# Attention and mixture of experts on one core: weight sums moved ahead of the signs, and four adds of the last pair moved from GpSimd to VectorE

## The chip, the cores and the metric

One core of one Trainium2 chip runs the whole kernel in one launch. The metric is the device time of an execution in microseconds (us); less is better. TensorE is called PE in the profile (PEld is its weight load), VectorE DVE, ScalarE ACT, GpSimd POOL and SyncE, which issues most DMAs, SP.

## What is computed

The inputs are `q`, `k`, `v` of shape (4, 8, 768, 64): four batches, eight heads, 768 tokens, 64 features. Attention is restricted by a hash, and a layer of eight experts follows:

```
bits   = (q @ proj > 0), (k @ proj > 0)        # 6 signs per token
mask   = bucket(q bits) == bucket(k bits)
scores = where(mask, q @ k.T / 8, -1e9)
attn   = softmax(scores)                       # over the keys
x      = (attn @ v), heads side by side        # 3072 tokens x 512
e      = argmax(x @ w_gate + modality_bias)    # one of 8 experts per token
out    = gate_weight * (relu(x @ w1[e]) @ w2[e])
```

## The kernel before, in words

**Attention.** The 32 heads are taken in 16 pairs, numbered 0 to 15; the variable `i` is the pair, `NPR` is 16 and `NT` is 6, the number of tiles of 128 tokens. The loop over pairs at the end of `attention` is software-pipelined. While pair `i` is scored and weighed, pair `i + 1` has its row maxima taken and pair `i + 2` is transposed and gets its hash signs. The order of TensorE's work inside a pair is written out by hand as six strings, one per key tile (`PLAN`; `PLAN0` for pair 0 and `LAST` for pair 15), and each letter is one step:

- S: a step of `score` (L410, L411): matmuls of one head's scores, 512 or 2 x 256 columns, into a PSUM bank; ScalarE takes the exponential into `pb` (L430, L444). From the second key tile on, the weights `pb` of each head are added up over the key tiles in `sp` (L447). There are ten such adds per pair, two for each of the key tiles 1 to 5. GpSimd does them; in pair 15 head 0 is on GpSimd and head 1 on VectorE (`spd=(15,)`).
- M: a step of `maxp` (L344, L350): matmuls whose row maxima VectorE takes (L346, L352). Two PSUM buffers.
- T: `turn`, three steps of transposes (L303), and as the fourth step `signs`: sixteen matmul instructions on tiles of 64 rows x 32 columns (L220) that write the two banks `psu`, and two VectorE comparisons that read these banks (L231).
- A: a third of `weigh`: two key tiles of weighted sums of `v` (L463), on tiles of 128 rows x 64 columns, into the same two banks `psu`. The first of a pair's three steps opens the banks with L457, which so has to wait for the comparisons of L231.
- Q: `sums(i - 1)`: four matmuls (eight instructions) on tiles of 128 rows x 32 columns (L486) that fold `sp` of the pair before into denominators, and one VectorE add into `gs` (L491). They read the result of the last adds of L447.
- V, v: sums of `v`. F, f, E, e, x, y: steps of `finish` and `finish_x`, which close a batch every four pairs, route its tokens and write rows of a table with indirect DMAs of GpSimd (L784). R: residues (L311, L312). B: the broadcast of maxima (L374 to L378). L, l: loads.

The order on TensorE in attention is fixed by these strings. On VectorE, ScalarE, GpSimd and SP a scheduler puts the instructions in order, by the order of emission and what each waits for; some are tied with `behind` or `after`, which order two instructions without a semaphore. `marks` holds the instructions that later code ties to.

**The seam.** `body` then starts the experts. The first slot `("e", 0)` (496 tokens of one expert, all from the first three batches) is prepared while pair 15 still runs: SP loads its rows of the table, GpSimd issues four gathers (L949), and `xprep` transposes the gathered rows in four chunks `c` of 128 features (L967), rounds them on ScalarE (L970) and takes the residue on VectorE (L974). The transposes of chunks 0 and 1 are tied behind the weighing of key tile 3, those of chunks 2 and 3 behind that of key tile 5, and the last third of the weighing behind the transposes of chunk 1. The experts' weights come as `raw`, are rounded by ScalarE (L929), and their residue is taken by VectorE or, for every second one of the first eight, by GpSimd (L933). The first matrix product is L985 to L987, the second L1026 to L1028. `finish(B - 1)`, which begins with `sums(NPR - 1)`, runs interleaved with this slot. Here the order on TensorE too is the scheduler's.

The lines that the change touches are the two plans, L447 in `score`, the letter Q in the loop of `attention` (L643), and the residue in `xprep` (L974).

Of the kernel before, what the change touches and what calls it, by code (L numbers as in the profile page):

```python
# [10 lines left out]
F32 = mybir.dt.float32  # L11
# [4 lines left out]
ALU = mybir.AluOpType  # L16
# [4 lines left out]
NT = S // 128  # L21
# [8 lines left out]
CFG = dict(spd=(15,), fxs=3, wy=(0.3, 0.71), hpf=0, he=0, hn=0, hm=0, avp=(1, 2, 3, 4, 5, 6), avs=(2,), early=2, w3=(0, 0.9), x3=(0, 1), nmd=1, man=(), man0=2, hpo=0, hpe=0, p0=(0, 1), p1=(0, 0.25), p2=(0, 0.4), p3=(0.4, 0.9), s0=4, rc='DDDD', rq=(1, 2), tq=(3, 3, 1, 1, 0, 0), wh=(0.5, 0.78), ws=(0.78, 1.05), n2=2, psx=2, psm=2, pss=2, npb=6, ut=8, qk=4, v=2, wm=(0, 0.9), wf=(0.04, 1.02), wx=(0.3, 0.71), sub="DPPD", fx='D', fx3='R', raw=4, wp=7, LS=4, LL=7, pn=8, rv=(0,), rs='DDPP', r1=(0, 0.5), r2=(0, 1), avg=1, fub=2, fd=2, pm=(), fj=0, fxe=1.0)  # L30
# [2 lines left out]
GROUP = 2  # L33
PLAN = (
    "yMSTSTMSM",
    "STEeLfvxMAVSSMMTxfe",
    "eySMSMlARRQfMSFMyF",
    "SRMSeMSMx",
    "SFfEMSfMRSMF",
    "fSMRSMMEBABSe",  # L40
# [9 lines left out]
LAST = (  # L50
    "SySS",
    "SevAVSSe",
    "eySSAQSy",
    "SSeS",
    "SSS",
    "SSASe",
# [32 lines left out]
def chain(*gens):  # L89
    for g in gens:  # L90
        yield from g


def attention(ctx, actx, tc, a, x_d, l_d, route=None, setup=None, before_last=None):
    nc = tc.nc
    q, k, v, proj = a["q"], a["k"], a["v"], a["proj"]
    NPR = a.get("npair", NP)
# [308 lines left out]
    marks = {}  # L406
# [6 lines left out]
    def score(i):  # L413

        t = st[i]
        t["sp"] = spool.tile([P, 2, S], F32, name="sp")
        t["pb"] = [pbuf[(NT * i + kt) % NPB] for kt in range(NT)]

        banks = [0]

        def bank(shape):
            banks[0] += 1
            if i == NPR - 1 and banks[0] % 2:
                return ps_m.tile(shape, F32, name="psm")
            return ps_s.tile(shape, F32, name="pss")

        def main(kt, h):
            sp = bank([P, MAIN])
            scores(t, sp, h, kt, COLS[0])
            marks["p"] = nc.scalar.activation(t["pb"][kt][:, h, 0:MAIN], sp, AF.Exp, scale=0.125).ins  # L430

        if i == 0:
            for kt in range(NT):
                main(kt, 0)
                yield
        for kt in range(NT):
            pb = t["pb"][kt]
            for h in range(int(i == 0), 2):
                main(kt, h)
                yield  # L440
            sp = bank([P, 2, REST])
            for h in range(2):
                scores(t, sp[:, h], h, kt, COLS[1])
            nc.scalar.activation(pb[:, :, MAIN:S], sp, AF.Exp, scale=0.125)  # L444
            if kt > 0:
                for h in range(2):
                    marks["add"] = (nc.vector if h and i in CFG["spd"] else nc.gpsimd).tensor_tensor(out=t["sp"][:, h], in0=(t["pb"][0] if kt == 1 else t["sp"])[:, h], in1=pb[:, h], op=ALU.add).ins  # L447
            yield

    def weigh():  # L450
# [135 lines left out]
    with tc.manual_schedule(engines={mybir.EngineType.PE}):  # L586
        load(1)
        load_v(0)
        load(2)
        constants()  # L590
        with tc.manual_schedule(engines={mybir.EngineType.DVE, mybir.EngineType.Activation, mybir.EngineType.Pool}):
            opening = first()
        wg = sm.tile([P, 4, 8], F32, name="wg", bufs=1)
        nc.sync.dma_start(out=wg, in_=a["moe_w_gate"].rearrange("(c p) e -> p c e", p=P))
        gst = fconst.tile([P, 4, 32], F32, name="gst")
        nc.gpsimd.memset(gst, 0.0)
        nc.gpsimd.tensor_copy(out=gst[0:64, :, 0:8], in_=wg[0:64])
        nc.gpsimd.tensor_copy(out=gst[64:128, :, 16:24], in_=wg[64:128])
        ones = fconst.tile([P, 4, 32], F32, name="ones")
        nc.gpsimd.memset(ones, 0.0)  # L600
        for c in range(4):
            nc.gpsimd.memset(ones[:, c, c:c + 1], 1.0)
        if setup is not None:
            setup()
        for nm in spread_to.values():
            nc.gpsimd.memset(nm.bitcast(F32), 0.0)
        avs = weigh()
        fins = xs = iter(())
        late = []
        for i in range(NPR):  # L610
            ss = score(i) if i else opening
            ms = maxp(i + 1, late) if i + 1 < NPR else iter(())
            ts = chain(turn(i + 2), signs(i + 2)) if i + 2 < NPR else iter(())
            rs = residues(i + 2) if i + 2 < NPR else iter(())
            if i % 4 == 0 and i > 0:
                fins = finish(i // 4 - 1)
            if i % 4 == 2 and i > 4:
                xs = finish_x(i // 4 - 1, 0, NT)
            for kt in range(NT):
                if i == NPR - 1 and kt == 1:  # L620
                    before_last(ps_x.tile([P, MAIN], F32, name="psx"))
                if i == NPR - 1 and kt < 3:
                    next(xs, None)
                    next(xs, None)
                for c in (PLAN0 if i == 0 else LAST if i == NPR - 1 else PLAN)[kt]:
                    if c == "S":
                        next(ss)
                    elif c == "M":
                        next(ms, None)
                    elif c == "T":  # L630
                        next(ts, None)
                    elif c == "R":
                        next(rs, None)
                    elif c == "A":
                        next(avs)
                    elif c == "B":
                        if late:
                            late.pop(0)()
                    elif c == "v":
                        vadds(i)  # L640
                    elif c == "V":
                        vsums(i)
                    elif c == "Q":  # L643
                        if i > 0:
                            sums(i - 1)
                    elif c == "L":
                        if i + 3 < NPR:
                            load(i + 3)
                    elif c == "l":
                        if i + 1 < NPR:  # L650
                            load_v(i + 1)
                    elif c == "F" and i % 4 == 0 or c == "f" and i % 4 == 1:
                        next(fins, None)
                    elif c == "e" and i % 4 >= 2 or c == "E" and i == NPR - 2:
                        next(fins, None)
                    elif c == "x" and i % 4 == 2 or c == "y" and i % 4 == 3:
                        next(xs, None)
                        next(xs, None)
        for _ in avs:
            pass  # L660
# [9 lines left out]
SL = sum(GW)  # L670
# [214 lines left out]
def experts(ctx, tc, a, x_d, tab, out, ps_x, idents, fold, marks):  # L885
    nc = tc.nc
# [16 lines left out]
    def after(ins, other):  # L903
        tc.add_manual_dep(ins, other.name, mybir.DependencyInfo(mybir.DependencyClass.NoSync, mybir.DependencyReason.DATA), reason="the first slot follows the last pair's steps")

    def nt(s):
        return 1 if s[0] == "s" else TS // P
# [44 lines left out]
    def xprep(s, xg, dst):  # L952

        xh = xp.tile([P, 4, TS], F32R, name="xh")
        xl = xp.tile([P, 4, TS], F32R, name="xl")
        dst += [xh, xl]
        if nt(s) == 1:
            tp = ps_x.tile([P, 4, P], F32, name="psx")
            for c in range(4):
                nc.tensor.transpose(tp.bitcast(F32R)[:, c], xg[:, 0, c * P:(c + 1) * P], identr)  # L960
            nc.scalar.copy(out=xh[:, :, 0:P], in_=tp)
            nc.vector.tensor_tensor(out=xl[:, :, 0:P], in0=tp, in1=xh[:, :, 0:P].bitcast(F32), op=ALU.subtract)
            return
        for c in range(4):
            tp = ps_x.tile([P, TS], F32, name="psx")
            for g in range(nt(s)):
                tr = nc.tensor.transpose(tp.bitcast(F32R)[:, g * P:g * P + GW[g]], xg[0:GW[g], g, c * P:(c + 1) * P], identr[0:GW[g], 0:GW[g]])  # L967
                if s == ("e", 0):
                    after(tr.ins, marks["u", 3 if c < 2 else 5])
            cp = nc.scalar.copy(out=xh[:, c, 0:SL], in_=tp[:, 0:SL])  # L970
            if s == ("e", 0) and c == 1:
                after(marks["U", 4], tr.ins)
                after(marks["ut"], cp.ins)
            nc.vector.tensor_tensor(out=xl[:, c, 0:SL], in0=tp[:, 0:SL], in1=xh[:, c, 0:SL].bitcast(F32), op=ALU.subtract)  # L974
            if c % 2:
                yield

# [268 lines left out]
```

## Time and profile before

| | us |
|---|---|
| median of 3 runs | 759.83 (759.24 to 761.26) |
| the profiled execution's own time | 760.22 |
| its span, first to last instruction | 758.1 |
| PE busy | 738.9 |
| DVE busy | 499.9 |
| POOL busy | 440.9 |
| ACT busy | 363.8 |

Times in the profile are counted from the start of the span. Pairs take some 26 to 29 us each; pair 15 ends at about 457 us, and the experts fill the rest. Matmuls are pipelined and their ends are modelled, so the distance from the start of one to the start of the next tells more than their durations. A row that stands for several instructions (x8) gives the time from the first one's start to the last one's end.

### The profile page before, as it was taken

Reading aid. Unit: us, or ns where it says so; the run is one execution under the profiler, and the core shown is the slowest. Engines: PE = TensorE matmul, PEld = TensorE weight load, DVE = VectorE, ACT = ScalarE, POOL = GpSimd, SP = SyncE. Lnnn points to the kernel's source line nnn. Section 1 sums busy time; section 2 is a strip of 40 time slices with the busy share of each in tenths; the row PEclk is TensorE's granted clock in tenths of the full one; section 3 lists DMA queues with packets and bytes.
Section 4 is the critical chain, followed back from the end, with each engine's and each line's share of the span. In section 5 each row is a group of like instructions: output and inputs, shape, how many; then the busy total and the mean of one; then the engine's idle time right before and its main releaser. Section 6 shows DMA issues by size and latency. Waiting matters only on the chain.

```text
span 758.1 us, 12219 instructions
## 1 busy us (share of the span) xinstructions
PE 738.9 (97%) x4308; PEld 523.4 (69%) x4308; DVE 499.9 (66%) x878; ACT 363.8 (48%) x649; POOL 440.9 (58%) x339
## 2 busy tenths in 40 slices
PE   6899999999999999999999999999999999999995
PEld 3556576566666657666666656888888877788884
DVE  6997779789877887977987877654343442334423
ACT  5446565555555555556465454343343432424333
POOL 8598779769888769887869984712222202202011
PEclk9999999999999999999999999999999999999998
DMA  9464455345676435664324163556544764434332
GB/s 187 116 142 109 113 122 140 83 106 116 111 131 162 105 91 133 121 157 124 92 69 85 61 199 112 115 207 185 159 137 139 250 214 147 141 123 139 96 113 82
DMA packets 105832, 99.26 MB, mean 131 GB/s; under 512 B 62594, under 2 KB 82978, under 8 KB 105760
## 3 DMA queue, kind: packets, MB, share of 16 engines
q1 hardware_dynamic: 99616, 83.79, 43.6%
q0 software_dynamic: 4832, 12.94, 4.9%
q10 hardware_dynamic: 1312, 1.65, 0.9%
q8 instruction: 36, 0.59, 0.4%
q14 instruction: 36, 0.29, 0.2%
HBM read 59.33 MB, written 12.94 MB: 95 GB/s over the span
## 4 chain that ended last, share of the span: by engine, by line
PE 81%; issue 9%; DMA 3%; POOL 2%; SPq 1%; DVE 1%; ACT 1%; POOLq 0%; ACTq 0%
PE psu L463 17%; PE pss L410 9%; PE pss L411 8%; PE psm L344 5%; PE hps L985 5%; PE hps L986 5%; PE hps L987 5%; PE yps L1026 4%; PE yps L1027 4%; PE yps L1028 4%; PE psm L350 3%; PE psx L303 2%; PE psx L486 2%; PE psx L548 2%; PE psu L220 1%
## 5 line engine op out<-in xcount | busy, mean ns | idle before, releaser
L447 POOL TENSOR_TENSOR sp<-sp,pb 128x768 f32<-128x768 f32 x124 | 225.3, 1851 | 14.1 <-ACT pb L444 13.4
L346 DVE TENSOR_REDUCE mx<-psm 128x1 f32<-128x512 f32 x192 | 130.0, 687 | 22.2 <-PE psm L344 19.1
L430 ACT ACTIVATE pb<-pss 128x512 f32<-128x512 f32 x186 | 111.5, 600 | 58.7 <-PE pss L411 50.2
L463 PE MATMUL psu<-pb,vt 128*64 128x512 f32 (+1 forms) x768 | 136.1, 497 | 0.0
L933 DVE TENSOR_TENSOR w<-raw,w 128x1024 fp32r<-128x1024 f32 x52 | 66.9, 1287 | 97.9 <-ACT w L929 97.3
L463 PEld LDWEIGHTS psu<-pb,vt 128*64 128x64 f32 x768 | 51.3, 137 | 70.6 <-issue 60.9
L929 ACT CAST w<-raw 128x1024 fp32r<-128x1024 f32 x56 | 58.5, 1047 | 81.4 <-PE yps L1028 76.7
L444 ACT ACTIVATE pb<-pss 128x512 f32<-128x512 f32 x93 | 55.6, 598 | 82.3 <-PE pss L411 80.0
L1096 POOL DMA_INDIRECT out<-y,tb x25 | 24.6, 984 | 104.1 <-ACT y L1095 100.4
L447 POOL TENSOR_TENSOR sp<-pb,pb 128x768 f32<-128x768 f32 x31 | 56.2, 1835 | 45.2 <-ACT pb L444 45.2
L1026 PE MATMUL yps<-w,hl 128*128 128x512 f32 x200 | 79.5, 397 | 0.0
L1027 PE MATMUL yps<-w,hh 128*128 128x512 f32 x200 | 78.1, 391 | 0.0
L1028 PE MATMUL yps<-w,hh 128*128 128x512 f32 x200 | 78.0, 390 | 0.0
L949 POOL DMA_INDIRECT xg<-x_d,tb x17 | 18.4, 1084 | 98.1 <-DMA tb<-tab 94.4
L985 PE MATMUL hps<-xh,w 128*128 128x496 f32 x192 | 74.4, 388 | 0.0
L986 PE MATMUL hps<-xl,w 128*128 128x496 f32 x192 | 73.8, 384 | 0.0
L987 PE MATMUL hps<-xh,w 128*128 128x496 f32 x192 | 73.8, 384 | 0.0
L410 PE MATMUL pss<-m_0g,s_0g 128*128 128x512 f32 (+1 forms) x186 | 69.2, 372 | 0.0
L991 DVE SCALAR_TENSOR_TENSOR hl<-hps,hh 128x496 fp32r<-128x496 f32 x48 | 32.4, 674 | 53.0 <-ACT hh L990 52.9
L352 DVE TENSOR_REDUCE mx<-psm 128x2 f32<-128x512 f32 x96 | 66.1, 688 | 1.0
L410 PE MATMUL pss<-m_1g,s_1g 128*128 128x512 f32 (+1 forms) x186 | 65.7, 353 | 0.2 <-ACT pb L430 0.2
L990 ACT ACTIVATE hh<-hps 128x496 fp32r<-128x496 f32 x48 | 28.1, 585 | 78.5 <-PE hps L987 76.1
(267 smaller groups left out, 1419.7 us busy)
## 6 DMA issues: line engine op xcount, KB each, us to landing
raw<-moe_w SPq DMA_DIRECT2D x56, 512.0 KB
vt<-v SPq DMA_DIRECT2D x16, 384.0 KB
qk<-q SPq DMA_DIRECT2D x31, 192.0 KB
qk<-k SPq DMA_DIRECT2D x31, 192.0 KB
x_d<-xs SPq DMA_DIRECT2D x18, 256.0 KB
tw<-moe_w SPq DMA_DIRECT2D x2, 2048.0 KB
m_0g<-m_0g SPq DMA_DIRECT2D x16, 192.0 KB
s_0g<-s_0g SPq DMA_DIRECT2D x16, 192.0 KB
```

What stands on the lines that cost most here:

```text
L346: marks["m"] = nc.vector.tensor_reduce(out=mx[:, qt + j, hi, 0:1], in_=mp, axis=AX.X, op=ALU.max).ins
L410: nc.tensor.matmul(out, t["s1"][h][:, ks], t["m1"][h][:, cs], start=True, stop=False)
L430: marks["p"] = nc.scalar.activation(t["pb"][kt][:, h, 0:MAIN], sp, AF.Exp, scale=0.125).ins
L447: marks["add"] = (nc.vector if h and i in CFG["spd"] else nc.gpsimd).tensor_tensor(out=t["sp"][:, h], in0=(t["pb"][0] if kt == 1 else t["s ...
L463: marks["u", kt] = nc.tensor.matmul(t["u"][part][64 * h:64 * h + 64, 0:w], t["v"][:, h, kt], t["pb"][kt][:, h, COLS[part]], start=False, s ...
L933: (nc.gpsimd if n < 8 and n % 2 else nc.vector).tensor_tensor(out=lo, in0=r, in1=hi.bitcast(F32), op=ALU.subtract)
L985: nc.tensor.matmul(hps, lo[:, c, fs], xh[:, c, 0:SL], start=(c == 0), stop=False)
L986: nc.tensor.matmul(hps, hi[:, c, fs], xl[:, c, 0:SL], start=False, stop=False)
L987: nc.tensor.matmul(hps, hi[:, c, fs], xh[:, c, 0:SL], start=False, stop=(c == 3))
L1026: nc.tensor.matmul(yps[g], hl[fc][:, gs], hi[:, fb], start=(fc == 0), stop=False)
L1027: nc.tensor.matmul(yps[g], hh[fc][:, gs], lo[:, fb], start=False, stop=False)
L1028: nc.tensor.matmul(yps[g], hh[fc][:, gs], hi[:, fb], start=False, stop=(fc == 7))
```

## The change

Three things are changed. The letter Q moves from the third string of `PLAN` to the second, to directly ahead of the T that is `signs`; this holds for pairs 1 to 13. Pairs 14 and 15, for which no signs are left to take, keep the old place under the letter q. In pair 15 the adds of head 0 from key tile 2 on go to VectorE, so that only the one of key tile 1 stays on GpSimd. And the two adds of key tile 5 of that pair are ordered behind the residue of chunk 1 of the first slot.

```diff
 PLAN = (
     "yMSTSTMSM",
-    "STEeLfvxMAVSSMMTxfe",
-    "eySMSMlARRQfMSFMyF",
+    "STEeLfvxMAVSSMMQTxfe",
+    "eySMSMlARRqfMSFMyF",
...
 LAST = (
     "SySS",
     "SevAVSSe",
-    "eySSAQSy",
+    "eySSAqSy",
...
             if kt > 0:
                 for h in range(2):
-                    marks["add"] = (nc.vector if h and i in CFG["spd"] else nc.gpsimd).tensor_tensor(out=t["sp"][:, h], in0=(t["pb"][0] if kt == 1 else t["sp"])[:, h], in1=pb[:, h], op=ALU.add).ins
+                    marks["add"] = (nc.vector if i == NPR - 1 and (h or kt > 1) else nc.gpsimd).tensor_tensor(out=t["sp"][:, h], in0=(t["pb"][0] if kt == 1 else t["sp"])[:, h], in1=pb[:, h], op=ALU.add).ins
+                    marks["add", kt, h] = marks["add"]
...
-                    elif c == "Q":
+                    elif c == "Q" and i < NPR - 2 or c == "q" and i >= NPR - 2:
                         if i > 0:
                             sums(i - 1)
...
-            nc.vector.tensor_tensor(out=xl[:, c, 0:SL], in0=tp[:, 0:SL], in1=xh[:, c, 0:SL].bitcast(F32), op=ALU.subtract)
+            sub = nc.vector.tensor_tensor(out=xl[:, c, 0:SL], in0=tp[:, 0:SL], in1=xh[:, c, 0:SL].bitcast(F32), op=ALU.subtract)
+            if s == ("e", 0) and c == 1:
+                for h in range(2):
+                    after(marks["add", NT - 1, h], sub.ins)
```

## Rows read from the trace of the kernel before

**Rows 1.** The page, busy tenths in 40 slices of the span.

```profile
PE   6899999999999999999999999999999999999995
```

**Rows 2.** Busy time by stretch: PE, PEld, DVE, ACT, POOL, granted clock, DMA share, GB/s.

```profile
450.00:452.40 2.40, 0.78 (x6) 0.32 (x4) 2.40 (x2) 0.60 (x1) 2.32 (x2) 1.00 0.19 73
453.90:457.30 3.40, 3.40 (x14) 1.11 (x10) 2.78 (x3) 2.33 (x3) 3.32 (x2) 0.50 0.11 42
```

**Rows 3.** Timeline of PE in pair 2: start, us, engine, line, operation, tiles.

```profile
83.66 2.80 PE L463 MATMUL psu<-pb,vt 128*64 128x512 f32 x16
86.39 0.49 PE L393 MATMUL psx<-va,ones 128*128 128x128 f32 x2
...
87.90 0.40 PE L350 MATMUL psm<-s_1g,m_1g 128*128 128x256 f32 x2
88.22 0.88 PE L220 MATMUL psu<-qk,zst 64*32 64x384 f32 x16
89.03 0.50 PE L410 MATMUL pss<-m_0g,s_0g 128*128 128x512 f32 x1
89.36 0.39 PE L411 MATMUL pss<-m_0g,s_0g 128*128 128x512 f32 x1
...
90.52 0.61 PE L457 MATMUL psu<-lone,vs 128*128 128x512 f32 x2
91.06 2.80 PE L463 MATMUL psu<-pb,vt 128*64 128x512 f32 x16
93.79 0.85 PE L486 MATMUL psx<-sp,ones 128*32 128x384 f32 x8
94.57 0.50 PE L350 MATMUL psm<-s_0g,m_0g 128*128 128x256 f32 x2
```

**Rows 4.** Timeline of PE in pair 7.

```profile
225.21 0.51 PE L457 MATMUL psu<-lone,vs 128*128 128x512 f32 x2
...
231.80 0.39 PE L350 MATMUL psm<-s_1g,m_1g 128*128 128x256 f32 x2
232.04 0.36 PE L410 MATMUL pss<-m_0g,s_0g 128*128 128x256 f32 x1
```

**Rows 5.** Waits of PE's weight loads, 60 to 437 us: total, times, longest.

```profile
PEld psu L457 <- DVE mask L231: 2.3, 9, 0.3
```

**Rows 6.** Timeline of POOL, the last two adds of pair 5.

```profile
190.45 3.60 POOL L447 TENSOR_TENSOR sp<-sp,pb 128x768 f32<-128x768 f32 x2
```

**Rows 7.** Timeline of PE, the signs of pair 6.

```profile
195.31 0.88 PE L220 MATMUL psu<-qk,zst 64*32 64x384 f32 x16
```

**Rows 8.** Timeline of DVE in pair 2.

```profile
89.42 1.26 DVE L231 TENSOR_SCALAR mask<-psu,thr 128x384 f32<-128x384 f32 x2
...
94.71 0.56 DVE L491 TENSOR_TENSOR gs<-gs,psx 128x384 f32<-128x384 f32 x1
```

**Rows 9.** Timeline of POOL: two of the first slot's gathers, one of the second's.

```profile
443.79 1.72 POOL L949 DMA_INDIRECT xg<-x_d,at  x1 [0.30 <-issue]
...
447.29 1.17 POOL L949 DMA_INDIRECT xg<-x_d,at  x1 [0.30 <-issue]
...
476.87 0.95 POOL L949 DMA_INDIRECT xg<-x_d,at  x1 [0.30 <-issue]
```

**Rows 10.** Timeline of DVE at the seam.

```profile
443.70 0.96 DVE L447 TENSOR_TENSOR sp<-sp,pb 128x768 f32<-128x768 f32 x1 [0.72 <-ACT pb L444]
...
451.32 2.57 DVE L447 TENSOR_TENSOR sp<-sp,pb 128x768 f32<-128x768 f32 x1
...
458.53 1.26 DVE L974 TENSOR_TENSOR xl<-psx,xh 128x496 fp32r<-128x496 f32 x2
```

**Rows 11.** Timeline of PE at the seam.

```profile
452.39 0.61 PE L967 MATMUL psx<-identr,xg 112*128 112x112 f32 x5 [0.36 <-DMA xg<-x_d,at]
...
459.80 0.85 PE L486 MATMUL psx<-sp,ones 128*32 128x384 f32 x8
```

**Rows 12.** Line L949, all gathers of the span.

```profile
DMA to landing us min/median/max: 3.5/4.1/7.3
```

## The prediction

> **What bounds the kernel now.** I read the page's 40 slices first. TensorE's row stands at 9 from the third slice to the last but one [rows 1], so from about 38 us to 740 us a matmul is always in the array. An instruction of another engine costs time only where it makes TensorE wait or drain. [...]
>
> Then I read TensorE's order in one pair of the middle, the third (pair 2) [rows 3]. Three small things cost time though the engine is never idle. A change of the array's tiling drains it: two matmuls of L350 take 0.32 us to the start of the signs (87.90 to 88.22), but 0.24 us where an untiled matmul follows (231.80 to 232.04) [rows 3, 4]. Behind the signs the next matmul of 512 columns needs 0.33 us to its successor (89.03 to 89.36), against some 0.23 for such a matmul inside a run. And L457, which overwrites the banks that hold the signs, is busy 0.61 us here and 0.51 us in pair 7 [rows 3, 4]: its weight load waits for VectorE's mask comparisons, nine times in the stretch [rows 5].
>
> **The change part by part.** (1) The sums' step of pairs 1 to 13 moves from behind the weighing to right before the signs. It issues four matmuls (eight instructions, 0.78 us from 93.79 to 94.57 [rows 3]) and one VectorE add, and no DMA, so no queue of SP or GpSimd sees it. The matmul work is the same in both places.
>
> Drains: before, the stream changes its tiling from weighing to sums, from sums to L350, from L350 to signs, and from signs to the next. After, from weighing to L350, L350 to sums, sums to signs, signs to the next. Four and four. Only the pair "sums to signs" is new, from columns of 32 over 128 rows to columns of 32 over 64 rows, and the trace has no such pair. Bounds: if it needs no drain, a tail of 0.08 us and a part of the head of 0.10 go, at most some 0.12 us per pair, 1.6 us over 13. If it costs a head on top (0.10 us for 128 columns of weights, so an estimate of 0.03 for 32), 0.4 us are lost. I take nothing, by the nearest row: weighing to sums also goes from one column tiling to another, and the sixteen weighing matmuls take 2.73 us before them (91.06 to 93.79) just as before an untiled matmul (83.66 to 86.39) [rows 3]. A change between two tilings drains like any other.
>
> Data: the sums read GpSimd's adds of the pair before. The moved step starts where the signs start now. The tightest of the 13 is pair 6: the adds of pair 5 end at 190.45 + 3.60 = 194.05 [rows 6], the signs start at 195.31 [rows 7], 1.26 us to spare. No wait.
>
> Masks: signs and L457 are both 0.78 us later behind the sums, so their distance stays. In pair 2 VectorE starts the two comparisons at 89.42, 0.39 us behind the end of the signs in TensorE's order, and its add of the sums, 0.56 us, at 94.71 [rows 8]. That add now stands ahead of the comparisons: they start at 89.98, take 1.26 us as before and end at 91.24, while L457 comes at 90.52 + 0.78 = 91.30. Before, they ended at 90.68 against 90.52. So the bubble of 0.10 us (0.61 less 0.51) closes, in the nine pairs that have it [rows 5]: 9 x 0.10 = 0.9 us gained. Bounds: 0 to 0.9. After that VectorE has the same work less the add, so later maxima come no later than now, within 0.1 us.
>
> Pairs 14 and 15 keep their place: they have no signs.
>
> (2) The last pair. Four adds leave GpSimd, where they stand behind the four gathers, and go to VectorE at 0.96 us each if nothing stands in their way [rows 10]. What they wait for stays: the exponentials. Who waits for them: only the sums of the last pair, at 459.80 on TensorE [rows 11]. GpSimd's next work, a split of the expert's weights, follows the gathers earlier. Both cost nothing under TensorE's matmuls.
>
> But VectorE's queue gets denser just where GpSimd issues the gathers. The second gather took 1.72 us, against 0.95 undisturbed; it starts at 443.79, inside VectorE's add from 443.70 to 444.66, and ends 0.85 after that add [rows 9, 10]. So a gather's issue waits until the add that it meets has ended. With two adds per key tile VectorE is full from 443.70 to about 449.2 (six of 0.96, a little overlapped). If the engines take turns, the third gather meets the add that ends at 446.5 and is done at 447.3, and the fourth starts at 447.6, meets the one that ends at 448.3 and is done at 449.2: 0.7 us later than now (447.29 + 1.17 = 448.46 [rows 9]). The gather of 447.29 is used at 452.39 [rows 9, 11], 5.1 us on, where the fastest in the kernel needs 3.5 [rows 12]; so 1.6 us of slack covers the 0.7, and I take 0 (bounds: nothing to +0.7, or the rival below). The turns are seen in the same place: VectorE's add of 451.32 took 2.57 us, 1.6 of it waiting, beside an add of GpSimd that had queued before it [rows 10].
> [...]
>
> (3) The last two adds follow the first slot's residues of chunk 1. Now one of them stands before these, at 451.32 [rows 10], so nothing is delayed ahead of the first matrix product. Behind the residues they push the next weight split and the residues of chunks 2 and 3 (458.53 now [rows 10]) by at most 1 to 1.5 us; TensorE uses chunk 2's only after the sums of 459.80, so after 460.6. Cost 0; without that cover, about 0.5 us.
>
> **Sum.** -0.9 us in the pairs, 0 at the seam. The profiled execution took 760.22 us (span 758.1 and 2.1 around it), which gives 759.3; it lies 0.39 above the median of the runs, 759.83, so on the median's scale I forecast **758.9 us**.
>
> **Rivals.** *Nothing comes of it*, 759.8: the comparisons stay late, because VectorE's queue is put in another order. For it: this order is not written out in the kernel. Chance 0.16.
> *Sums and signs run together without a drain*, 758.9 - 1.6 = 757.3. For it: both use columns of 32; against it: weighing to sums. Chance 0.20.
> [...] The 3.4 us at 0.50 cost 1.7 us [rows 2]: 757.2 or less. [...] Chance 0.08.
> *The gathers are locked out* (the slower side): GpSimd gets no turn between VectorE's back-to-back adds. Then the second gather's issue ends at 449.2 + 0.8 = 450.0, and the fourth starts at 450.0 + 2 x 0.3 + 0.95 = 451.6; landing 3.5 later gives 455.1 in place of 452.4, +2.7 us, and up to 1.7 more if the half-clock stretch doubles: 761.6 to 763.3. It decides from a fourth issue later than 452.4 - 3.5 = 448.9. Against it: the turns above. Chance 0.12.
>
> **How the numbers follow.** The forecast has 0.44. A measurement of this kernel can tell about 0.3%, 2.3 us, from no change, so most of this is "same". Faster by more: half of the case without a drain and the closed hole, 0.18. Slower: most of the lock-out, 0.11. The rest is 0.71. The range goes from 756.8 (most of the two fast cases) to 761.6 (the first bound of the slow one).
>
> **What would show it.** In the changed profile: sums right ahead of signs with no "POOL sp" wait; L457 busy 0.51 us in all pairs; the pitch from the sums' first matmul to the signs' first still 0.78 us (0.66 would mean that no drain is there); the fourth gather starting at about 447.6 and the transposes ending their wait within 0.7 us of now, measured from the last scores; a stretch at 0.50 of about 3.4 us. I am wrong if the hole at the seam changes by over 1 us, or if TensorE idles between 60 and 440 us.

## The result, and the profile after

The changed kernel takes **762.8 us** (median of 11 runs, 760.35 to 765.37), the kernel before 758.48 beside it (11 runs, 757.7 to 761.26): ratio **1.006, 95% interval 1.0047 to 1.0073**. It is slower, by about twice what a measurement can tell from no change. The forecast was 758.9, with a range to 761.6.

The profiled execution took 763.01 us, with a span of 761.1 against 758.1. The page of the changed kernel, first the busy tenths in 40 slices, then the shares of the chain of waits by engine:

```profile
PE   6899999999999999999999997999999999999995
...
PE 80%; issue 10%; DVE 5%; POOL 2%; DMA 2%; ACT 1%; POOLq 0%; SPq 0%; ACTq 0%; DVEq 0%
```

Against [rows 1] a 7 stands in the 25th slice, 457 to 476 us, and VectorE now holds 5% of the chain. Lines behind L447 up to L974 are one higher than before (L457 is L458, L486 is L487, L933 is L934, L974 is L975), and the first matrix product is L989 to L991. Three stretches of the changed kernel, columns as in [rows 2]:

```profile
450.20:452.60 2.40, 1.68 (x13) 1.08 (x13) 0.32 (x2) 1.23 (x3) 0.00 (x0) 1.00 0.50 95
457.85:461.69 3.84, 0.00 (x1) 0.00 (x0) 3.84 (x3) 0.00 (x0) 2.12 (x1) 1.00 0.42 137
462.10:465.60 3.50, 3.50 (x17) 2.36 (x9) 0.84 (x3) 0.00 (x0) 0.00 (x0) 0.51 0.90 300
```

The hole at the seam, the first stretch of [rows 2], has shrunk: 1.68 us busy of 2.40 instead of 0.78, and the granted clock is 1.00 in it and up to the sums, where the second stretch of [rows 2] has 0.50. In its place TensorE stands still for 3.84 us from 457.85, and from 462.1 to 465.6 the granted clock is 0.51. The timeline of PE in the changed kernel: pair 2, pair 10, and the seam.

```profile
88.11 0.40 PE L350 MATMUL psm<-s_1g,m_1g 128*128 128x256 f32 x2
88.44 0.85 PE L487 MATMUL psx<-sp,ones 128*32 128x384 f32 x8
89.22 0.88 PE L220 MATMUL psu<-qk,zst 64*32 64x384 f32 x16
90.02 0.50 PE L410 MATMUL pss<-m_0g,s_0g 128*128 128x512 f32 x1
90.36 0.39 PE L411 MATMUL pss<-m_0g,s_0g 128*128 128x512 f32 x1
...
91.51 0.51 PE L458 MATMUL psu<-lone,vs 128*128 128x512 f32 x2
91.95 2.80 PE L464 MATMUL psu<-pb,vt 128*64 128x512 f32 x16
94.68 0.50 PE L350 MATMUL psm<-s_0g,m_0g 128*128 128x256 f32 x2
...
311.91 0.40 PE L411 MATMUL pss<-m_0g,s_0g 128*128 128x512 f32 x1
312.80 0.50 PE L344 MATMUL psm<-s_1g,m_1g 128*128 128x512 f32 x1 [0.49 <-DVE mx L352]
...
452.19 2.80 PE L464 MATMUL psu<-pb,vt 128*64 128x512 f32 x16
...
461.69 1.10 PE L487 MATMUL psx<-sp,ones 128*32 128x384 f32 x8 [3.84 <-DVE xl L975]
```

Pair 2 is as forecast. Pair 10 holds a stop that the kernel before does not have. At the seam the sums of pair 15 wait for VectorE's residue of chunk 2: they need a PSUM bank `psx`, of which there are two, and it still holds that chunk's transposes. The timeline of DVE in the changed kernel: pairs 2, 6 and 10, then the seam.

```profile
89.63 0.56 DVE L492 TENSOR_TENSOR gs<-gs,psx 128x384 f32<-128x384 f32 x1
90.19 1.26 DVE L231 TENSOR_SCALAR mask<-psu,thr 128x384 f32<-128x384 f32 x2
...
200.02 0.96 DVE L312 TENSOR_TENSOR s_0g<-qk,m_0g 128x768 fp32r<-128x768 f32 x1
200.90 0.95 DVE L312 TENSOR_TENSOR s_1g<-qk,m_1g 128x768 fp32r<-128x768 f32 x1
...
308.87 2.14 DVE L312 TENSOR_TENSOR s_0g<-qk,m_0g 128x768 fp32r<-128x768 f32 x1
310.93 1.21 DVE L312 TENSOR_TENSOR s_1g<-qk,m_1g 128x768 fp32r<-128x768 f32 x1
312.07 0.68 DVE L352 TENSOR_REDUCE mx<-psm 128x2 f32<-128x512 f32 x1
...
452.57 1.26 DVE L975 TENSOR_TENSOR xl<-psx,xh 128x496 fp32r<-128x496 f32 x2 [2.08 <-ACT xh L971]
453.74 4.01 DVE L447 TENSOR_TENSOR sp<-sp,pb 128x768 f32<-128x768 f32 x2
457.68 3.38 DVE L934 TENSOR_TENSOR w<-raw,w 128x1024 fp32r<-128x1024 f32 x1
460.98 1.24 DVE L975 TENSOR_TENSOR xl<-psx,xh 128x496 fp32r<-128x496 f32 x2
```

The two last adds take 4.01 us, where two take about 1.9 by [rows 10]. Before them VectorE has nothing to do for 2.08 us, the time in which the order holds them back. And the timeline of POOL in the changed kernel, same stretches:

```profile
201.63 1.08 POOL L384 TENSOR_TENSOR va<-vt 128x384 f32<-128x384 f32 x1 [1.33 <-DMA vt<-v]
...
309.17 1.02 POOL L384 TENSOR_TENSOR va<-vt 128x384 f32<-128x384 f32 x1
310.26 1.07 POOL L385 TENSOR_TENSOR va<-va 128x128 f32<-128x128 f32 x1
...
443.92 0.97 POOL L950 DMA_INDIRECT xg<-x_d,at  x1 [0.30 <-issue]
445.19 1.51 POOL L950 DMA_INDIRECT xg<-x_d,at  x1 [0.30 <-issue]
447.01 1.43 POOL L950 DMA_INDIRECT xg<-x_d,at  x1 [0.30 <-issue]
...
454.05 2.89 POOL L934 TENSOR_TENSOR w<-raw,w 128x1024 fp32r<-128x1024 f32 x1 [5.61 <-ACT w L930]
457.63 2.34 POOL L934 TENSOR_TENSOR w<-raw,w 128x1024 fp32r<-128x1024 f32 x1 [0.70 <-ACT w L930]
```

GpSimd's weight residue of 454.05 runs to 456.94. VectorE's first add is done at about 454.7; the second ends at 457.75, 0.81 us behind GpSimd, so it did almost all its work after GpSimd had finished. The next pair does the same: VectorE's weight residue, 1.22 us alone, takes 3.38 beside GpSimd's of 457.63. So the residue that frees the bank comes at 460.98.

**The balance of the two profiled executions.** To the first step that moves (the signs of 62.32 before, the sums of 62.61 after) the new one is 0.29 us later. From there to the last L457 or L458 (438.26 and 438.61) both hold the same work, 14 sums among it: 375.94 and 376.00 us, +0.06. From there to the end of the span 319.84 and 322.49, +2.65. That is the 3.0 us. The medians lie 4.3 us apart; the profiled execution of the kernel before, 760.22 us, is 1.7 above its median of 758.48.

Two questions follow: why the pairs give nothing, and what stands in the seam.

### The profile page after: what moved, and what is told of

It reads as the page before. It is cut to its first block, busy times and chain, and to the rows that moved or that the text cites. A ratio compares the mean times of both kernels' runs of the same rounds, so it can differ in the third digit from the quotient of the medians.

```text
span 761.1 us, 12234 instructions
## 1 busy us (share of the span) xinstructions
PE 738.7 (97%) x4308; PEld 524.6 (69%) x4308; DVE 499.5 (66%) x882; ACT 363.4 (48%) x649; POOL 430.4 (57%) x335
## 4 chain that ended last, share of the span: by engine, by line
PE 80%; issue 10%; DVE 5%; POOL 2%; DMA 2%; ACT 1%; POOLq 0%; SPq 0%; ACTq 0%; DVEq 0%
PE psu L464 15%; PE pss L410 9%; PE pss L411 8%; PE psm L344 5%; PE hps L989 5%; PE hps L990 5%; PE hps L991 5%; PE yps L1030 4%; PE yps L1031 4%; PE yps L1032 4%; PE psm L350 3%; PE psx L303 2%; PE psx L487 2%; PE psu L220 2%; PE psx L549 1%
## 5 line engine op out<-in xcount | busy, mean ns | idle before, releaser
L447 POOL TENSOR_TENSOR sp<-sp,pb 128x768 f32<-128x768 f32 x120 | 216.4, 1836 | 12.6 <-ACT pb L444 12.2
L464 PE MATMUL psu<-pb,vt 128*64 128x512 f32 (+1 forms) x768 | 134.4, 492 | 0.0
L934 DVE TENSOR_TENSOR w<-raw,w 128x1024 fp32r<-128x1024 f32 x52 | 65.9, 1267 | 93.6 <-ACT w L930 62.6
L464 PEld LDWEIGHTS psu<-pb,vt 128*64 128x64 f32 x768 | 50.9, 136 | 70.8 <-issue 61.8
L447 POOL TENSOR_TENSOR sp<-pb,pb 128x768 f32<-128x768 f32 x31 | 56.3, 1835 | 46.2 <-ACT pb L444 46.2
L989 PE MATMUL hps<-xh,w 128*128 128x496 f32 x192 | 74.5, 389 | 0.0
L991 PE MATMUL hps<-xh,w 128*128 128x496 f32 x192 | 74.1, 387 | 0.0
L410 PE MATMUL pss<-m_0g,s_0g 128*128 128x512 f32 (+1 forms) x186 | 69.0, 371 | 0.0
L410 PE MATMUL pss<-m_1g,s_1g 128*128 128x512 f32 (+1 forms) x186 | 66.0, 355 | 0.2 <-ACT pb L430 0.2
```

Source lines behind the costliest of these rows:

```text
L410: nc.tensor.matmul(out, t["s1"][h][:, ks], t["m1"][h][:, cs], start=True, stop=False)
L447: marks["add"] = (nc.vector if i == NPR - 1 and (h or kt > 1) else nc.gpsimd).tensor_tensor(out=t["sp"][:, h], in0=(t["pb"][0] if kt == 1 ...
L464: marks["u", kt] = nc.tensor.matmul(t["u"][part][64 * h:64 * h + 64, 0:w], t["v"][:, h, kt], t["pb"][kt][:, h, COLS[part]], start=False, s ...
L989: nc.tensor.matmul(hps, lo[:, c, fs], xh[:, c, 0:SL], start=(c == 0), stop=False)
L991: nc.tensor.matmul(hps, hi[:, c, fs], xh[:, c, 0:SL], start=False, stop=(c == 3))
```

## The experiments

Each ran beside the kernel before on the same chip. "Pairs" is the stretch just named (375.94 before, 376.00 after), "last product to sums" the time from the last L457 or L458 to the first L486 or L487 of pair 15 (21.54 and 23.08), and a pitch is the time from L457 of one pair to L457 of the next. The expectations speak of "first to last masked product", which has pair 0's pitch in it; that one varies by 0.9 us between executions with the move (24.4 to 25.3) and is left out of "pairs". The two other profiles with the sums at their old place, further down, have pairs of 375.69 and 375.61 us, so some 0.3 us of a difference from 375.94 is chance.

**The move of the sums alone.**

```diff
-  ...(nc.vector if i == NPR - 1 and (h or kt > 1) else nc.gpsimd)
+  ...(nc.vector if h and i in CFG["spd"] else nc.gpsimd)
...
-            if s == ("e", 0) and c == 1:
-                for h in range(2):
-                    after(marks["add", NT - 1, h], sub.ins)
```

> Only the move of the sums; the adds of the last pair as in the kernel before. Theory A (the loss is made at the seam by the adds alone): no stop of TensorE ahead of the last sums, the pairs from the first L457 to the last within 1 us of the kernel before (397.6 us), time 757.5 to 759.5, that is within 1 us of the kernel before. Theory B (the moved sums cost several us in the pairs, through VectorE's later maxima): pairs at 399 us or more, time 760 to 763.

Measured: 758.81 us, ratio 1.0005 (0.9995 to 1.0015). Last product to sums 20.12 us; no stop over 0.31 us behind the hole, and a granted clock of 1.00 from 434 to 472 us. The slowdown is not in the move. But the pairs took 376.68 us, 0.74 more than before, where 0.9 less was forecast.

**The adds and their order alone.** The plans and the letter Q as before:

```diff
-                    elif c == "Q" and i < NPR - 2 or c == "q" and i >= NPR - 2:
+                    elif c == "Q":
```

> Only the adds of the last pair and their order behind the residue; the sums in their old place. Theory A: TensorE stops for 3 to 4.5 us ahead of the last sums, while VectorE's two last adds and a weight split wait for GpSimd's splits, and the time is 761.5 to 764. Theory B: at most 1 us of a stop, time 758 to 759.5.

Measured: 761.86 us, ratio 1.0047 (1.0033 to 1.006). The slowdown is here. In its profiled execution, the shortest of its five (758.75), TensorE had no stop before the sums, although VectorE's two adds took 3.97 us here too. From 448 to 456 us, with the hole in it, the mean granted clock was 0.79 (1.00 in the first profile of the change), and the sixteen matmuls of L464 took 4.50 us from 451.60 (2.80 from 452.19 there). With that TensorE came to the sums later, and VectorE's next weight residue met nothing (1.21 us), because GpSimd's second one began only at 458.67. So this profile does not show where the loss of the median lies; the stop behind two such meetings is seen in the profiles of the change.

**The change without the order.** Only the three lines with `after(marks["add", ...], sub.ins)` are taken out.

> The changed kernel without the order of the two last adds behind the residue of chunk 1. Theory A1 (the place of these adds makes the loss): they run at about 451 to 453 us, in a stretch in which VectorE is idle in the changed kernel and GpSimd has no split yet; 0.96 us each; the stop ahead of the last sums falls from 3.8 to under 1 us and the time to 757 to 759.5. Theory A2 (it is GpSimd's earlier weight splits that hold VectorE's split of the third block up, wherever the adds stand): the stop stays at 2 us or more, time 760.5 to 763.

Measured: 758.05 us, ratio 0.9988 (0.9978 to 0.9997). Against the change (1.006) three lines are worth 0.72%, 5.5 us. The profile of the change priced them at 5.6: 3.84 of stop and half of the 3.5 us at a granted clock of 0.51. From the last product to the end the two profiled executions differ by 4.65 us (322.49 and 317.84): without the order a stop of 0.67 us ahead of the sums is left, behind the same residue, and the hole is longer (1.57 us of stops). The timeline of DVE in this kernel, and behind the dots that of POOL:

```profile
451.96 1.83 DVE L447 TENSOR_TENSOR sp<-sp,pb 128x768 f32<-128x768 f32 x2 [0.63 <-ACT pb L444]
454.17 1.26 DVE L975 TENSOR_TENSOR xl<-psx,xh 128x496 fp32r<-128x496 f32 x2 [0.38 <-ACT xh L971]
...
455.64 2.38 POOL L934 TENSOR_TENSOR w<-raw,w 128x1024 fp32r<-128x1024 f32 x1 [6.35 <-ACT w L930]
```

The adds now lie in the time in which VectorE waits for the gathered rows, before GpSimd has a weight residue to take, and cost 1.83 us for two.

**The change without GpSimd's weight residues.** The order stays; GpSimd fills the residues of the weight blocks 1 and 3 with zeros, so that this kernel leaves that part of the first matrix product out.

```diff
+        if n in (1, 3):
+            nc.gpsimd.memset(lo.bitcast(F32), 0.0)
+        else:
```

> The changed kernel, where GpSimd fills the residues of the weight blocks 1 and 3 with zeros instead of computing them (this leaves that part of the first product out): GpSimd reads no SBUF there. If VectorE is held up by GpSimd's splits, its two last adds take 0.96 us each, its split of block 2 1.2 us, the residue of chunk 2 starts some 3.5 us earlier than in the changed kernel, the stop ahead of the last sums is under 0.5 us and the time 756.5 to 758.5. If it is the length of VectorE's queue alone (two adds more in front of the split), the stop stays over 2.5 us and the time over 760.5.

Measured: 757.78 us, ratio 0.9997 (0.9984 to 1.0009). Timeline of DVE at the seam in this kernel:

```profile
454.03 1.82 DVE L447 TENSOR_TENSOR sp<-sp,pb 128x768 f32<-128x768 f32 x2
455.77 1.22 DVE L937 TENSOR_TENSOR w<-raw,w 128x1024 fp32r<-128x1024 f32 x1
456.90 1.25 DVE L978 TENSOR_TENSOR xl<-psx,xh 128x496 fp32r<-128x496 f32 x2
```

GpSimd's fills are done by 452.45, ahead of these rows. Same order, same instructions on VectorE, but 1.82 instead of 4.01 and 1.22 instead of 3.38; the sums start at 458.08, with no stop. So it is not the length of VectorE's queue: it is GpSimd's residue beside it.

**The change once more,** to see whether one profile's stop was an accident.

> The changed kernel once more, for a second profile of the seam. Theory A (the two last adds behind the first slot's residues stand beside GpSimd's weight residue and take over 3.5 us, TensorE stops before the sums or is slowed ahead of them): stop over 2 us before the sums, or a fall of the granted clock ahead of it; last masked product to first sums 21 to 23.2 us (20.3 in the version without the order, 21.5 before). Rival (the 3.84 us of the first profile was one run's accident): stop under 1 us and no fall, under 20.6 us.

Measured: 763.69 us in one run; the timeline of PE in this execution has the same stop, to a hundredth of a us:

```profile
461.46 1.51 PE L487 MATMUL psx<-sp,ones 128*32 128x384 f32 x8 [3.85 <-DVE xl L975]
```

The granted clock falls to 0.50 here too, but for longer, from about 460.7 to 467.4 us; two stretches behind the stop, columns as in [rows 2]:

```profile
461.70:465.10 3.40, 3.40 (x14) 1.77 (x7) 0.84 (x2) 0.00 (x0) 0.00 (x0) 0.50 0.87 290
465.10:467.40 2.30, 2.30 (x8) 1.91 (x7) 1.35 (x6) 0.58 (x1) 0.00 (x0) 0.50 0.08 30
```

Last product to sums 22.97 us. The pairs took 377.29 here, 1.35 more than before, against 0.06 in the first profile. So the pairs vary, and the next runs are about them. Their pitches fall on a few values:

| pitch, us | pair 2 | pair 6 | pair 7 | pair 10 | pair 11 |
|---|---|---|---|---|---|
| before | 25.90 | 27.21 | 26.22 | 27.07 | 26.23 |
| after, first profile | 25.81 | 27.13 | 26.24 | 27.83 | 26.85 |
| after, second profile | 25.80 | 27.86 | 26.84 | 27.82 | 26.84 |
| the move alone | 25.81 | 27.83 | 26.23 | 27.83 | 26.85 |

The plain pairs gain 0.09. Pairs 6, 7, 10 and 11, in which a batch is closed, lose 0.6 to 0.8 or nothing. In pairs 6 and 10 the loss holds a stop of 0.49; in pair 11 of the change it is two shorter pauses behind VectorE's maxima, ahead of the products of L344 at 340.65 and 342.44.

**The sums moved, but not in those four pairs** (no order, adds on VectorE):

```diff
-  elif c == "Q" and i < NPR - 2 or c == "q" and i >= NPR - 2:
+  elif c == "Q" and i not in (6, 7, 10, 11, 14, 15) or c == "q" and i in (6, 7, 10, 11, 14, 15):
```

> Both of the last pair's heads added on VectorE from the third key tile on, no order behind the residues, and the sums next to the signs in all pairs but those worked on in steps 6, 7, 10, 11 (there they stand behind the masked product as before). Theory A (the move costs its time only where the rounds that sum v over both engines run, because VectorE's add of the sums now stands ahead of the masks and the residue): the pitches that were 27.83, 27.83 and 26.85 us come back to 27.07, 27.07 and 26.22, the two stops of .49 at 202.9 and 312.5 us of the span are gone, the others keep 25.82, 28.58, 26.91; first to last masked product 396.3 to 396.8 us, the median 1.5 to 2.3 us under that with the sums moved everywhere (ratio to the kernel before .996 to .9975, 755.6 to 756.9). Theory B (the slower pairs come from something else that the moved sums change, a phase of a queue or the pairs before them): pitches stay within .2 of 27.8 and the time within .4 us of the run with the sums moved everywhere (.9988).

Measured: 756.0 us (754.92 to 757.72), ratio **0.9973** (0.9964 to 0.9983). The pairs took 374.56 us, 1.38 less than before (1.1 less than the two other profiles with the old place), and no stop over 0.05 us is left between 60 and 440 us. The loss does sit in these four. First to last masked product came to 395.89 us. The pitches of pairs 6 and 10 are 27.09 and 27.06, as expected; that of pair 11, 27.00, holds the 0.78 us of a second step of sums (its own and that of pair 12, which stands in the new place), and pairs 5 and 9 have none in turn.

**VectorE's add at its old place.** The first theory was that VectorE's add of the sums, 0.56 us, now stands ahead of the masks and makes what follows late.

```diff
+        elif hold:
+            held.append((b, g))
...
+                    elif c == "q":
+                        late_sum()
```

> As the version without the order (adds of the last pair on VectorE, sums next to the signs everywhere), but VectorE's add of the sums into the collected ones is issued at its old place, behind the masked product; the bank of the sums is held until then. The first of every four pairs, where it is a copy and not an add, is as in the change. Theory A (VectorE's order, not TensorE's, makes the slow pairs): pitches 27.07, 27.07, 26.22 in pairs 6, 10, 11, 25.82 and 28.58 in the others, so about as the version that moves the sums in the other pairs only: ratio .996 to .9975. Theory B (TensorE's order makes them: the maxima's products come .78 us later in the pair): pitches of 27.8 stay, and the time is within .4 us of .9988; a third outcome is that the held bank makes the transposes wait, which would show as stops on the products into that bank with VectorE's add as releaser, and a pitch over 25.9 in the plain pairs.

Measured: 758.54 us, ratio 1.0005 (0.9987 to 1.0023), stops of 0.50 and 0.51 as before. This decides nothing: VectorE's add still runs ahead of the masks and the residue (195.80 in pair 6, the residue at 199.48), so the order under test is that of the change without the order, measured a second time. Pair 7 came out at 26.86 this time and at 26.23 in the other, so the same order takes both.

**VectorE's add held behind the residue,** this time by a tie, in the version without the order.

```diff
+            if h == 1 and i in (8, 12, 13):
+                behind(marks["gs"], res)
```

> The version without the order (sums next to the signs everywhere), with VectorE's add of the sums held behind the second q/k residue in steps 6, 10 and 11, where it stood before. In the runs so far the add ended at 196.35 us and the masks began at 196.36, .09 behind the end of the signs at 196.27. Theory B (the order of TensorE makes the slow pairs: it comes to the maxima's products .78 us sooner after the signs, while GpSimd's sum of v, whose start hangs on the scores ahead of the sums, now starts with VectorE's first residue): masks and the first residue start no earlier than now (within .1 us of 4.0 after the signs), the first residue still takes over 2 us, VectorE's add then comes on top, the stops of .49 grow to .8 to 1.05 and the pitches of pairs 6 and 10 to 28.1 to 28.4. Theory A (VectorE's add ahead of the masks makes them): residues take .99 and 1.93 again, no stop, pitches 27.0 to 27.1.

Measured: 759.73 us, ratio 1.0029 (1.0017 to 1.0041); the stops in pairs 6 and 10 grew to 0.96, their pitches to 28.23 and 28.19, and pair 11 has a stop of 0.52. Timeline of DVE in pair 6 of this kernel, and behind the dots that of PE:

```profile
199.58 2.14 DVE L312 TENSOR_TENSOR s_0g<-qk,m_0g 128x768 fp32r<-128x768 f32 x1
201.65 1.21 DVE L312 TENSOR_TENSOR s_1g<-qk,m_1g 128x768 fp32r<-128x768 f32 x1
202.78 0.54 DVE L495 TENSOR_TENSOR gs<-gs,psx 128x384 f32<-128x384 f32 x1
...
203.98 0.50 PE L347 MATMUL psm<-s_1g,m_1g 128*128 128x512 f32 x1 [0.96 <-DVE mx L355]
```

The first theory falls. With the add out of the way the residue starts no earlier (the masks wait for the signs) and still takes 2.14 us; the add then comes on top. What takes its time is the residue's neighbour on GpSimd.

**Without GpSimd's sum of v.** A fill with zeros takes the place of its three adds, so this kernel leaves that common part of some masked products out. GpSimd runs these adds one pair ahead of their letter, so the fill fell into pairs 5, 9 and 10; pair 10 is the test, and pair 11 keeps its adds.

```diff
+        if i in (6, 10, 11):
+            nc.gpsimd.memset(a2, 0.0)
+        else:
```

> The version without the order, with GpSimd's three adds of the sum of v over the tokens replaced by a fill with zeros in steps 6, 10 and 11; the masked products of these pairs then lack their common part, so this kernel leaves out part of the computation. Theory B with GpSimd's share (the residue of 2.14 us waits for GpSimd's add of v, and without it TensorE doesn't stop): residues .99 each, no stop at 203 and 312 us, pitches of pairs 6, 10, 11 of 26.9 to 27.0, 26.9 to 27.0 and 26.1 to 26.2. Rival (TensorE coming .78 sooner is enough by itself): residues shorter, but stops of .2 or more stay.

Measured: 756.32 us in one run. Timeline of DVE in pairs 10 and 11 of this kernel:

```profile
308.55 0.96 DVE L312 TENSOR_TENSOR s_0g<-qk,m_0g 128x768 fp32r<-128x768 f32 x1
309.42 0.95 DVE L312 TENSOR_TENSOR s_1g<-qk,m_1g 128x768 fp32r<-128x768 f32 x1
...
335.70 2.15 DVE L312 TENSOR_TENSOR s_0g<-qk,m_0g 128x768 fp32r<-128x768 f32 x1
```

Pair 10 has no stop and a pitch of 27.15 (0.2 above what was expected); pair 11, with GpSimd's adds, keeps 2.15 us and 26.84. In pair 6 the table of v landed late in this run, GpSimd waited for it, and there was no stop either, as in the first profile of the change (`L384` there at 201.63 behind a wait of 1.33, both residues under 1 us). So the slow pitch comes where GpSimd's add meets VectorE's first residue. The other profiles bear it out: eight move the sums in all these pairs, and of their 32 pairs 6, 7, 10 and 11 the 23 with a first residue of 2.14 to 2.17 us have the slow pitch, the 9 with 0.96 us do not.

**The adds alone, no order, sums at the old place.**

```diff
-  ...(nc.vector if h and i in CFG["spd"] else nc.gpsimd)
+  ...(nc.vector if i == NPR - 1 and (h or kt > 1) else nc.gpsimd)
```

> The kernel before with one edit: VectorE adds both heads of the last pair from the third key tile on, with no order behind the residues and the sums at their old place. Theory A (the adds by themselves are harmless and take GpSimd's wait out of the end of the pair; the order is what cost): pairs as before (25.90, 27.07), adds at about 452 us in VectorE's idle stretch, 1.8 us for two, no fall of the granted clock and no stop over .8 us in the seam between pairs and first GEMM; ratio .996 to .998. Theory B (the adds on VectorE take its time from the weight residues and maxima of the last pair, order or not): a stop over 1.5 us ahead of the sums or the first GEMM, ratio 1.000 to 1.004.

Measured: 757.97 us, ratio 0.9997 (0.9987 to 1.0008): neither a cost nor a gain, so both theories missed on the ratio. The adds took 1.83 us for two, as expected, but the hole was there, and the granted clock behind it was 0.50 from 454 to 456 us in this execution.

**The limited move with and without the adds.** The first is the kernel before with nothing but the condition on `i`, the second repeats the best kernel beside it.

> The kernel before with one edit: sums next to the signs in all pairs but those worked on in steps 6, 7, 10, 11; the last pair's adds stay on GpSimd and VectorE as before. Theory A (the pairs give the gain, the adds on VectorE next to nothing): first to last masked product 395.8 to 396.3 us, the time within .5 us of the kernel with both, ratio .997 to .9985. Theory B (the adds carry half of the gain or more): the time stands 1 us or more above the kernel with both.

> The limited move with the last pair's adds on VectorE and no order, once more beside the kernel without those adds. Theory A: ratio .9964 to .9983 again, within .5 us of the kernel without the adds. Theory B: 1 us or more under it.

Measured: 757.39 us, ratio 0.9988 (0.9974 to 1.0003) without the adds, 755.97, ratio **0.9972** (0.9959 to 0.9984) with them. Their pairs agree (374.49 and 374.53; first to last masked product 396.62 and 396.53, above what was expected), so the 1.4 us between them lie at the seam, from the last L458 to the end 318.47 and 316.61 us. This speaks for the second theory. Together with the adds alone, worth nothing with the old place, the adds' worth is open between 0 and 1.4 us. The version with both beats the kernel before and the change, in two measurements.

## Why the prediction was wrong

**Drains (part 1): right.** Sums to signs 0.78 us (88.44 to 89.22), the tail of L350 0.33 (88.11 to 88.44) as the 0.32 of [rows 3], weighing to L350 2.73, and the successor of L410 behind the signs 0.34. The new change of tiling cost what the old ones do; the rival of 1.6 us did not come.

**Data and masks (part 1): right.** The comparisons end at 90.19 + 1.26 = 91.45 ahead of L458 at 91.51, which is busy 0.51 instead of 0.61 [rows 3]; the plain pitch falls from 25.90 to 25.81.

**"Later maxima come no later than now, within 0.1 us": wrong.** It counted VectorE's instructions and took their durations as fixed. In the version with the sums at the old place (the adds and their order alone) the timeline of DVE, and behind the dots that of POOL, has in pair 6:

```profile
198.89 0.99 DVE L312 TENSOR_TENSOR s_0g<-qk,m_0g 128x768 fp32r<-128x768 f32 x1
199.80 1.93 DVE L312 TENSOR_TENSOR s_1g<-qk,m_1g 128x768 fp32r<-128x768 f32 x1
...
199.89 1.01 POOL L384 TENSOR_TENSOR va<-vt 128x384 f32<-128x384 f32 x1
```

The first residue is done at 199.88, when GpSimd's add of v begins. GpSimd's queue hangs on the exponentials ahead of the sums, VectorE's residue on the signs behind them. Sums that go in between push VectorE 0.78 us back against GpSimd, and the first residue meets GpSimd's adds (308.87 against 309.17 in the change). At the same time 0.78 us of matmuls is gone between the weighing and the maxima's products, so TensorE asks for VectorE's maxima that much sooner. Without the meeting VectorE is still in time (27.13 to 27.16 with no stop), with it TensorE stops for 0.49. So the term of -0.9 us measured +0.06 in the first profile and +0.70 to +1.35 in the others that move all thirteen and change nothing else in the pairs.

**The gathers (part 2): right, smaller.** They take turns with VectorE's adds (1.51 and 1.43 us, against 0.95 undisturbed [rows 9]); the last is done at 448.44, as before (448.46), not 0.7 later. The lock-out did not come. The hole, though, did shrink in this profile: 1.68 us busy of 2.40, a granted clock of 1.00 from 438.61 to 455.62, and the first matrix product 17.01 us behind the last L458 instead of 19.80 behind L457 (458.06 before), 2.79 gained. The forecast gave a closed hole 0.08, but by the profiles the gain goes with the kernel: from the last L457 or L458 to the first matrix product the nine profiles with both the move and VectorE's adds take 16.6 to 17.4 us, the two with the move alone 18.2, the three with the sums at their old place 19.3 to 19.8. How the moved sums reach the seam was not tried.

**"At most 1 to 1.5 us ... Cost 0" (part 3): the step that failed.** Three things were wrong in it. The push was not the adds' own 1.9 us: held back behind the residues they met GpSimd's weight residue, which the forecast itself had let come earlier, and grew to 4.01 us, and the next weight residue to 3.38. The cover was read the wrong way round: "TensorE uses chunk 2's only after the sums", but the sums take the bank that chunk 2's residue frees. The trace of before shows how thin it was: that residue, the first of the two at 458.53 [rows 10], took 0.66 us, to about 459.2, and the sums started at 459.80 [rows 11], so there were 0.6 us to spare. And behind the stop of 3.84 us the granted clock was 0.51 for 3.5 us, another 1.7 (3.0 in the second profile). So 0 measured 5.5, of which the smaller hole hid 2.8.

**The rivals** for the slower side named the gathers' issue; the loss came by the same kind of blocking between the same two engines, at another place. Of the two signs that would prove the forecast wrong, an idle TensorE between 60 and 440 us is there (0.49 at 312.80); the hole changed by 0.9 us in its own stops and by 2.8 with the clock behind it.

## What to carry to other kernels

Before an order ties an instruction behind another, look at what the other engine does at the later time: here two adds of VectorE took 1.83 us in a stretch in which GpSimd was idle, and 4.01 us beside a weight residue of GpSimd of 2.89 us (1.82 in the same place without it). When a step is moved on one engine, ask which queues hang on what lies ahead of it and which on what lies behind; the two shift against each other, even if each does the same work. And follow a PSUM bank to its next owner: a wait for a bank can turn "used only after" round.

## What was not expected of the hardware

TensorE's granted clock fell to 0.50 at the stops of 3.84 and 3.85 us in both profiles of the change, for 3.3 us in the first (from 462.2, 0.5 us behind the stop) and for 6.7 us in the second (from 460.7, still in the stop). All 11 timed runs of the change show a mean clock of 0.988 to 0.993, where those of the kernel before range from 0.992 to 0.999, but for one of 0.945 (764.54 us). Behind the hole of the seam the clock falls in some executions only: it did in the three profiles with the sums at their old place (the kernel before with stops of 1.62 us in all, the adds and their order alone with 1.24, the adds alone with 1.80), and in none of the eleven that move the sums, though the change without the order has 1.57 and the limited move alone 0.58 there and another 1.12 us ahead of the transposes of 454.50. So the length of the stops alone does not decide. What does was not tried, and neither was why the hole is 0.7 us long in some profiles and 1.6 in others; a gain of 2 us at the seam can hang on it.

The wait between VectorE and GpSimd also works at the scale of small instructions: GpSimd's third add of v, 128 x 128 elements, takes 0.46 us alone (203.32 in pair 6 of the change's first profile) and 1.05 beside a residue (311.41 in pair 10). Which engine waits can't be told from the recorded starts. In pair 10 of the change the residue starts 0.30 us ahead of GpSimd's add (308.87 and 309.17) and is the one that waits (2.14 and 1.02 us); in pair 5 of the kernel before the starts are 0.29 us apart (172.39 and 172.68), and it is GpSimd's add that waits (1.14 and 1.72 us).
